# Weight preparation beside the matmuls: stores issued later, one shared ring of tiles, finer hand-out

## Chip, cores and metric

The kernel runs on one core of one Trainium2 chip. The metric is the device time of one execution in microseconds (us), lower is better. TensorE multiplies matrices, VectorE and ScalarE do element-wise work, GpSimd a few additions, and SyncE issues nearly all DMAs. In profiles they are PE (PEld its weight loads), DVE, ACT, POOL and SP (SPq its queue).

## The reference

Windowed attention, then a gated layer, then a second layer, all in float32 on 3072 tokens of width 512:

```python
# attention: 4 batches, 8 heads, 768 tokens, head dim 64, in chunks of 32 queries;
# keys: 8 memory keys, 16 to the left, the chunk, 8 to the right
a = np.exp(scores - max); a = a / (sum + 1e-9); out = a @ v_full
# gated layer, d_ff 1536
x = (sigmoid(x @ w_gate) * (x @ w_val)) @ w_out
# second layer, d_ff 2048
h = x @ w_in; out = (h * sigmoid(h)) @ w_out2
```

The weights arrive as 64-bit floats, and the kernel stages each weight as pairs of 32-bit words and makes its 32-bit value out of them.

## The kernel before

**Precision and products.** A float32 operand is split into an upper part (a cast on ScalarE) and a lower part (the difference, on VectorE); a product is three matmuls, upper x upper, upper x lower, lower x upper. Feature-major 128x512 tiles are multiplied by 128x128 weights.

**Gated layer** (the loop over `BLOCKS1`). Four blocks of 512 tokens, 12 rounds of 128 hidden features each. One round is 12 matmuls for the gate (`pg`), 12 for the value (`pv`), and 12 for the output of the round before (`emit_out1`). Three times a round, `steps(i)` runs attention's work that is due there (`run_events`) and lets the preparation go on. In the first block the gated layer's own weights are staged (`Feed`); from the second block on, output weights are reloaded from DRAM (`load_wo`), and `Pace` prepares operands. Attention has 24 tiles of 128 tokens. From tile 8 on, each takes two rounds: "meet" (context of the tile before, line 309, scores, line 221, maximum, subtraction and exponent, lines 258 to 270), two steps later "norm" (sum and reciprocal, lines 277 to 279, and eight ScalarE multiplications, line 286), four steps after the meet "turn" (four TensorE transposes, line 293, and a copy, line 294).

**Two more strips.** The last 1024 of the 3072 tokens pass the gated layer as the strip with index -1; then the second layer takes the 3072 tokens in three strips of 1024 (0, 1, 2). Both use a seven-product scheme on halves of each matrix, so their weights are needed as seven combined blocks. First products (`pair2`): each pair of hidden tiles takes seven products (A11, S1, S2, A12, S3, S4, A22, six matmuls each), summed into banks `c1`, `c2`, `c3`, which copies and additions (lines 980, 984, 922, 985) read between products: `c1` after product 1 by ScalarE, `c3` after product 2 by ScalarE, `c2` after products 3 and 5 by VectorE. Strip -1 has six pairs, each with a gate half and a value half (the value half multiplies on VectorE, line 974); strips 0 to 2 have eight pairs. After an odd pair a closing subtraction and split is done in the next one (`tail`, `form`). Then come second products (`out2`). The loads of combined weights (`next_granule`, five buffers) are issued as each buffer is used up.

**Preparation.** The combined weights are made on the chip and stored to DRAM. `PairC` makes those of the gated layer (gate, value, and output weights "o"), `Pair2` those of the second layer: of the input weights in the gated layer's blocks 1 to 3, of the output weights in the first products of strips -1 and 0. A `Pair2` loads two tiles (`stg`), changes the exponent range of their upper words on ScalarE ("rebias", line 125), joins words on VectorE (lines 135 and 138), makes four sums (line 627), and then for four operand tiles an upper part (ScalarE, line 97), a lower part (VectorE, line 100) and a store (lines 728 and 734). `prepare` is a generator over these pieces, each with an assumed cost; `Pace.go(us)` adds to a budget and takes pieces until it is spent. In the gated layer it gets 1.8 us per step, less attention's share; in the strips 3.0 after each half pair (`PREPC`) or pair (`PREPL`). Staged tiles have a ring of four; operand tiles have three buffers in the gated layer and two in the strips. A store is issued right behind its lower part. For an output weight of the gated layer, `reach` starts the pair when its even member is about to be multiplied, and line 668 adds the upper and lower parts of both members.

All engines run their queues in order, and the order is the one in which the program issues (`manual_schedule`).

Of the kernel before, what the change touches and what calls it, by code (L numbers as in the profile page):

```python
# [51 lines left out]
DVE_US = {"meet": 2.1, "norm": 1.0}  # L52
PREP1 = 1.8
PREPC = 3.0
PREPL = 3.0
# [3 lines left out]
def moe_kernel(ctx: ExitStack, tc: tile.TileContext, qh, kh, vh, wg, wv, wo, w2i, w2o, out):  # L59
# [52 lines left out]
    class Unit:  # L112
        def __init__(self, src, name, slot=None, keep=None):
            self.src, self.name, self.slot, self.keep = src, name, slot, keep
            self.pool = None

        def load(self):
            pool = self.pool or p1
            self.stg = pool.tile([P, 512, 2], I32, tag="stg", name=f"stg_{self.name}", bufs=4)
            return nc.sync.dma_start(out=self.stg.rearrange("p a b -> p (a b)"), in_=self.src)  # L120
# [267 lines left out]
    with tc.manual_schedule():  # L388
# [197 lines left out]
        events = {}  # L586
        for t in range(n0, NTILE + 1):
# [30 lines left out]
        def sums_of(f32s, order):  # L618
            at = {o: n for n, o in enumerate(order)}
            for o, a, b, op in (  # L620
# [5 lines left out]
                o, a, b = at[o], at[a], at[b]  # L626
                nc.vector.tensor_tensor(out=f32s[:, o], in0=f32s[:, a], in1=f32s[:, b], op=op)

        def co_tile(pool, name, bufs):
            co = pool.tile([P, 2, 512], F32R, tag="co", name=name, bufs=bufs)  # L630
            return co.rearrange("p a (m k) -> p a m k", m=2)

        class PairC:
# [3 lines left out]

            def load(self):
                if self.k != "o":
                    self.src = [w_t[2 * self.p + j][:, "gv".index(self.k)] for j in range(2)]  # L640
                    return
                self.src = None

            def early(self):
                return (1 + self.p % 2, 2 * self.p + 1) not in wo_u
# [13 lines left out]
            def steps(self):  # L659
                if self.k == "o":  # L660
                    bi = 1 + self.p % 2
                    even, odd = (wo_u[bi, 2 * self.p + j] for j in range(2))
                else:
                    even, odd = self.src
                f32s = p1.tile([P, 8, 256], F32, tag="f", name=f"fc{self.k}{self.p}")
                v = f32s.rearrange("p m c -> p (m c)")
                for o, w in ((v[:, :512], even), (v[:, 1536:], odd)):
                    nc.vector.tensor_tensor(
                        out=o, in0=w[:, 0].bitcast(F32), in1=w[:, 1].bitcast(F32), op=ALU.add
                    )  # L670
                if self.k == "o":
                    order = (A11, A21, S1, S2, S3, S4, A12, A22)
                else:
                    self.store(A11, even)
                    order = (A11, A12, S1, S2, S3, S4, A21, A22)
                    self.store(A22, odd[:, :, 256:])
                yield 1.4
                sums_of(f32s, order)
                yield 1.45
                for c, ids in enumerate(((S1, S2), (S3, S4))):  # L680
                    co = co_tile(p1, f"cc{self.k}{self.p}_{c}", 3)
                    split(co[:, 0], co[:, 1], f32s[:, 2 + 2 * c : 4 + 2 * c], nc.vector)
                    yield 0.7
                    if self.k == "o":
                        for n, i in enumerate(ids):
                            self.store(i, co[:, :, n])
                    else:
                        self.store(ids[0], co)

        class Pair2:  # L690

            def __init__(self, k, p, pool, bufs):
                self.k, self.p, self.pool, self.bufs = k, p, pool, bufs
                w = w2i if k == "i" else w2o
                self.units = [Unit(w[f], f"w2{k}{f}") for f in (2 * p, 2 * p + 1)]
                for u in self.units:
                    u.pool = pool

            def early(self):
                return False  # L700

            def load(self):
                for u in self.units:
                    u.load()

            def steps(self):
                k, p = self.k, self.p
# [12 lines left out]
                sums_of(f32s, range(8))  # L720
                yield 1.45
                for c in range(4):
                    m = min(2, 7 - 2 * c)
                    co = co_tile(self.pool, f"co{k}{p}_{c}", self.bufs)[:, :, :m]
                    split(co[:, 0], co[:, 1], f32s[:, 2 * c : 2 * c + m], nc.vector)
                    yield 0.7 if m == 2 else 0.4
                    if k == "i":
                        nc.sync.dma_start(
                            out=w2i_d[p, :, c // 2, :, 2 * (c % 2) : 2 * (c % 2) + m],
                            in_=co.bitcast(F32),  # L730
                        )
                    else:
                        for j in range(m):
                            nc.sync.dma_start(
# [562 lines left out]
```

## Time and profile before

| | us |
|---|---|
| median of 3 runs | 1213.25 (1208.88 to 1215.08) |
| the profiled execution | 1213.65, span 1211.9 |
| TensorE busy | 1125.5 |
| VectorE / ScalarE / GpSimd busy | 764.0 / 563.1 / 70.0 |

The profile is of one execution. "Busy" is the time in which an engine executes; in a line of waits, the engine before the arrow stood idle until the one behind it released it. In rows of the timeline the bracket at the end gives the idle time just before and what ended it. The granted clock (PEclk) is TensorE's, 1.00 for the higher of two levels.

### The profile page before, as it was taken

What the parts mean: (1) busy time and instruction counts of PE and PEld (TensorE: products, weight loads), DVE (VectorE), ACT (ScalarE), POOL (GpSimd) and SP (SyncE); (2) the same over time, 40 slices, a digit from 0 to 9 for tenths busy, and PEclk for the clock granted to TensorE, in tenths of its full rate; (3) what the DMA queues carried; (4) which work ended last, traced back from release to release, by engine and by line L of the source; (5) the groups of instructions that cost most, each with busy time, mean ns of one, the idle gap of its engine ahead of it and who ended that gap; (6) DMA issues with size and microseconds to landing.
All of it is one profiled execution on the core that took longest, in us unless ns stands there. A gap on an engine that the chain in (4) does not pass through costs nothing. (4 is left out here: it accounts for less than half of the span.)

```text
span 1211.9 us, 19021 instructions
## 1 busy us (share of the span) xinstructions
PE 1125.5 (93%) x7580; PEld 904.8 (75%) x7580; DVE 764.0 (63%) x1140; ACT 563.1 (46%) x919; POOL 70.0 (6%) x50
## 2 busy tenths in 40 slices
PE   7999999998899999877888996789999999999998
PEld 4888877776787777765666785668888888888887
DVE  7888756675566666455465974436873468734565
ACT  6766655554546553322223553335534445444442
POOL 0000000000000000011010101110001100011000
PEclk9999999998999999988888998889999999999999
DMA  8887777786676977656678767567575575755552
GB/s 300 286 296 271 242 274 251 261 274 235 241 260 236 342 270 269 211 196 212 234 261 272 263 220 240 165 203 292 187 247 183 191 302 178 246 194 186 224 198 95
DMA packets 106248, 288.03 MB, mean 238 GB/s; under 512 B 8624, under 2 KB 39344, under 8 KB 95408
## 3 DMA queue, kind: packets, MB, share of 16 engines
q1 hardware_dynamic: 105872, 286.43, 68.0%
q8 instruction: 60, 0.98, 0.3%
q10 hardware_dynamic: 288, 0.39, 0.1%
q14 instruction: 28, 0.23, 0.1%
HBM read 210.24 MB, written 76.55 MB: 237 GB/s over the span
## 5 line engine op out<-in xcount | busy, mean ns | idle before, releaser
L957 PE MATMUL c<-xp,wr 128*128 128x512 f32 x1008 | 237.6, 398 | 22.1 <-ACT s L980 20.2
L957 PEld LDWEIGHTS c<-xp,wr 128*128 128x128 f32 x1008 | 193.6, 193 | 65.5 <-ACT s L980 21.4
L1089 PE MATMUL o<-gf,wr 128*128 128x512 f32 x1008 | 229.0, 389 | 0.0
L1089 PEld LDWEIGHTS o<-gf,wr 128*128 128x128 f32 x1008 | 189.2, 188 | 39.3
L360 PE MATMUL pv<-x,w 128*128 128x512 f32 x564 | 143.8, 405 | 5.3 <-DVE sg L375 5.3
L360 PE MATMUL pg<-x,w 128*128 128x512 f32 x564 | 136.7, 391 | 1.3 <-ACT x L97 1.3
L100 DVE TENSOR_TENSOR gf<-g,gf 128x1024 fp32r<-128x1024 f32 x84 | 103.8, 1239 | 47.5 <-ACT gf L97 47.0
L360 PEld LDWEIGHTS pv<-x,w 128*128 128x128 f32 x564 | 107.1, 194 | 31.7 <-DVE sg L375 8.5
L97 ACT CAST gf<-g 128x1024 fp32r<-128x1024 f32 x84 | 88.1, 1052 | 86.8 <-PE o L1089 71.5
L360 PEld LDWEIGHTS pg<-x,w 128*128 128x128 f32 x564 | 104.9, 188 | 24.9 <-ACT x L97 3.5
L922 DVE TENSOR_TENSOR s<-c,s 128x512 f32<-128x512 f32 x48 | 33.2, 691 | 71.3 <-PE c L957 71.3
L377 ACT CAST g<-sg 128x512 fp32r<-128x512 f32 x48 | 29.8, 620 | 96.4 <-DVE sg L375 96.4
L97 ACT CAST coo<-fo 128x512 fp32r<-128x512 f32 (+1 forms) x32 | 17.5, 562 | 101.5 <-DMA w2o_d<-coo 67.8
L928 ACT ACTIVATE g<-s 128x512 f32<-128x512 f32 x48 | 30.3, 632 | 60.8 <-DVE s L922 60.8
L925 DVE TENSOR_TENSOR g<-g,g 128x1024 f32<-128x1024 f32 x48 | 58.4, 1216 | 0.0
L985 POOL TENSOR_TENSOR s<-s,s 128x512 f32<-128x512 f32 x24 | 37.4, 1559 | 348.2 <-ACT s L984 297.3
L100 DVE TENSOR_TENSOR coo<-fo,coo 128x512 fp32r<-128x512 f32 (+1 forms) x32 | 19.4, 623 | 53.6 <-ACT coo L97 53.6
L380 DVE TENSOR_TENSOR g<-sg,g 128x512 fp32r<-128x512 f32 x48 | 33.1, 689 | 24.8 <-ACT g L377 24.8
L286 ACT ACTIVATE e<-e,r 128x64 f32<-128x64 f32 x136 | 34.4, 335 | 28.4 <-DVE r L279 28.3
L922 DVE TENSOR_TENSOR u<-c,s 128x512 f32<-128x512 f32 x24 | 16.5, 688 | 39.9 <-PE c L957 38.0
L105 PE MATMUL y<-g,wor 128*128 128x512 f32 x144 | 40.1, 400 | 0.0
L270 ACT ACT_TABLE_LOAD x21 | 26.9, 1283 | 25.8 <-DVE e L262 23.9
(593 smaller groups left out, 1647.7 us busy)
## 6 DMA issues: line engine op xcount, KB each, us to landing
wr<-w2o_d SPq DMA_DIRECT2D x42, 1024.0 KB, 4.8
wr<-w2i_d SPq DMA_DIRECT2D x24, 1024.0 KB, 5.5
wor<-wo_d SPq DMA_DIRECT2D x36, 512.0 KB, 6.0
wr<-w2i_d SPq DMA_DIRECT2D x24, 768.0 KB, 4.5
w2o_d<-coo SPq DMA_DIRECT2D x56, 256.0 KB, 4.5
w2i_d<-coi SPq DMA_DIRECT2D x24, 512.0 KB, 3.8
wr<-wc_d SPq DMA_DIRECT2D x12, 1024.0 KB, 6.0
v<-in_vh_dram SPq DMA_DIRECT2D x21, 512.0 KB, 6.3
```

The source lines that it names most:

```text
L97: nc.scalar.copy(hi, src)
L100: lo_eng.tensor_tensor(out=lo, in0=src, in1=hi.bitcast(F32), op=ALU.subtract)
L105: nc.tensor.matmul(o, w_hi, x_hi, start=first, stop=False)
L286: nc.scalar.activation(out=e[:, g], in_=e[:, g], func=AF.Copy, scale=r[:, g])
L360: nc.tensor.matmul(o[:, :n], w[:, pw, kt * P : (kt + 1) * P], x[kt][:, px, :n], start=i == 0, stop=i == len(steps) - 1,)
L380: nc.vector.tensor_tensor(out=g[:, 1, :n], in0=sg[:, :n], in1=g[:, 0, :n].bitcast(F32), op=ALU.subtract)
L922: nc.vector.tensor_tensor(out=o, in0=a, in1=b_, op=ALU.add)
L925: nc.vector.tensor_tensor(out=o, in0=a, in1=b_, op=ALU.subtract)
L928: nc.scalar.activation(out=o, in_=i, func=AF.Silu)
L957: nc.tensor.matmul(o, w[:, pw, m, kt * P : (kt + 1) * P], X[i][:, px, kt], start=first and j == 0, stop=j == 5, skip_group_check=not first,)
L985: nc.gpsimd.tensor_tensor(out=s5, in0=s5, in1=s1, op=ALU.add)
L1089: nc.tensor.matmul(c[at[i], dp], w[:, pw, pl, dp * P : (dp + 1) * P], f[:, px, pl], start=i in (A11, S1, S2) and pp == 0 and j == 0, stop= ...
```

## The change

- **One ring.** Staged tiles and operand tiles share one tag: seven tiles in the gated layer, six in the strips (before, 4 + 3 and 4 + 2).
- **Late stores.** A store is put in a list behind its lower part and issued four calls of `go` later, or earlier if a new operand tile is asked for while four (in the strips three) stores are in the list.
- **Pieces apart.** After the rebias, and after the first upper parts, the call of `go` ends, so that joins and lower parts come at least one call later; upper parts are made two operand tiles ahead. The budget is held to 2.5 us. A pair's staged tiles are loaded behind the sums of the pair before.
- **Fine hand-out.** In the strips, `go(0.9)` is called inside `pair2` after every second product, in place of 3.0 after each pair.
- **Output weights of the gated layer.** `begin` adds both members when the odd one is about to be multiplied; the rest follows as the next item.
- **Attention.** From tile 8 on the exponent is issued one step after the subtraction, and the normalisation is one VectorE multiplication (line 288) instead of eight ScalarE ones. Assumed costs and budgets are set anew.

```diff
-DVE_US = {"meet": 2.1, "norm": 1.0}
-PREP1 = 1.8
-PREPC = 3.0
-PREPL = 3.0
+DVE_US = {"meet": 2.1, "norm": 1.75}
+PREP1 = 1.95
+PREP2 = 0.9
...
+                if fast:
+                    events.setdefault(at + 1, []).append(("exp", t))
...
-                        steps += list(att_scores(t, sx, e_tile(t)))
+                        more = list(att_scores(t, sx, e_tile(t)))
+                        if t >= 2 * n0:
+                            exps[t] = more.pop()
+                        steps += more
...
+                elif what == "exp":
+                    exps.pop(t)()
...
-                    att_norm(t, nc.scalar if t >= 2 * n0 else nc.vector)
+                    att_norm(t)
...
         def co_tile(pool, name, bufs):
-            co = pool.tile([P, 2, 512], F32R, tag="co", name=name, bufs=bufs)
-            return co.rearrange("p a (m k) -> p a m k", m=2)
+            co = pool.tile([P, 512, 2], I32, tag="stg", name=name, bufs=bufs)
+            co = co.rearrange("p a b -> p (a b)").rearrange("p (h m k) -> p h m k", h=2, m=2)
+            return co.bitcast(F32R)
...
+            def begin(self, even, odd):
+                self.t = [t_slot(f"tc{self.p}_{j}") for j in range(2)]
+                self.whole(self.t[0], even)
+                self.whole(self.t[1], odd)
...
         class Pair2:
...
-                for j, u in enumerate(self.units):
-                    u.rebias()
+                for u in self.units:
+                    u.rebias()
+                yield None
...
-                sums_of(f32s, range(8))
-                yield 1.45
+                sums_of({i: f32s[:, i] for i in range(8)})
+                if self.after is not None:
+                    self.after.load(pace)
+                yield 1.5
+                cos = []
+
+                def high(c):
+                    m = min(2, 7 - 2 * c)
+                    co = pace.co(self.pool, f"co{k}{p}_{c}")[:, :, :m]
+                    nc.scalar.copy(co[:, 0], f32s[:, 2 * c : 2 * c + m])
+                    cos.append(co)
+
+                high(0)
+                high(1)
+                yield None
                 for c in range(4):
-                    m = min(2, 7 - 2 * c)
-                    co = co_tile(self.pool, f"co{k}{p}_{c}", self.bufs)[:, :, :m]
-                    split(co[:, 0], co[:, 1], f32s[:, 2 * c : 2 * c + m], nc.vector)
-                    yield 0.7 if m == 2 else 0.4
...
+                    lo_of(cos[c], f32s[:, 2 * c : 2 * c + cos[c].shape[2]])
+                    pace.later(lambda c=c, co=cos[c]: self.store(c, co))
+                    if c + 2 < 4:
+                        high(c + 2)
+                    yield 0.7 if c < 3 else 0.4
...
         class Pace:
+            LAG = 4
...
+            def co(self, pool, name):
+                while len(self.fifo) >= self.cap:
+                    self.fifo.pop(0)[1]()
+                return co_tile(pool, name, self.bufs)
+
+            def later(self, store):
+                self.fifo.append((self.step, store))
...
             def go(self, us):
-                self.due += us
...
+                self.step += 1
+                while self.fifo and self.fifo[0][0] <= self.step - self.LAG:
+                    self.fifo.pop(0)[1]()
+                self.due = min(self.due + us, 2.5)
+                while self.due > 0:
+                    cost = self.advance()
+                    if cost is None or cost is False:
                         break
+                    self.due -= cost
+
+            def begin(self, item, *args):
+                item.begin(*args)
+                self.due -= 1.4
+                self.urgent.append(item)
...
                 if i in final:
                     next_granule()
+                if b < 0 or b == 0 and p < NPAIR - 2:
+                    beats[0] += 1
+                    if beats[0] % 2 == 0:
+                        prep.go(PREP2)
...
-                    if pending[0] in (1, 2) and pending[1] % 4 == 2 * pending[0] - 2:
-                        prep.reach(("o", pending[1] // 2))
+                    if pending[0] in (1, 2):
+                        seen[pending[1]] = wo_u[pending]
+                        if pending[1] % 4 == 2 * pending[0] - 1:
+                            q = pending[1] // 2
+                            prep.begin(PairC("o", q), seen[2 * q], seen[2 * q + 1])
...
-        prep = Pace([Pair2("o", p, pool, 2) for p in range(NPAIR)])
+        prep = Pace([Pair2("o", p, pool) for p in range(NPAIR)], 6, 3)
```

## Rows read from the trace of the kernel before

**Rows 1.** Page, first part: an engine's busy time, share of the span, instructions.
```profile
PE 1125.5 (93%) x7580; PEld 904.8 (75%) x7580; DVE 764.0 (63%) x1140; ACT 563.1 (46%) x919; POOL 70.0 (6%) x50
```
**Rows 2.** Table by stage: from:to and length, busy us, then granted clock, DMA share, GB/s.
```profile
149.76:486.29 336.53, 318.03 (x3106) 250.17 (x3105) 213.11 (x403) 173.73 (x341) 0.00 (x0) 0.98 0.75 265
494.44:661.67 167.23, 133.98 (x517) 105.20 (x516) 89.69 (x143) 49.01 (x87) 18.94 (x12) 0.90 0.69 238
661.67:720.43 58.76, 57.62 (x254) 47.38 (x253) 54.05 (x55) 31.31 (x35) 4.28 (x2) 1.00 0.69 232
720.43:827.13 106.70, 84.64 (x338) 67.60 (x337) 43.21 (x66) 39.02 (x65) 13.46 (x8) 0.87 0.64 209
827.13:1208.06 380.93, 380.92 (x1681) 314.89 (x1679) 232.93 (x236) 167.59 (x213) 32.64 (x22) 1.00 0.60 211
```
**Rows 3.** Chain that ended last, in order of time: start us, us, what.
```profile
730.83 9.50 DMA w2o_d<-coo
...
740.66 1.23 ACT stg_w2o L125 x2
...
903.29 76.16 PE c L957 x336
```
**Rows 4.** TensorE's waits: us in total, times, longest us.
```profile
PE c L957 <- ACT s L980: 20.2, 3, 8.4
PE sx L309 <- ACT at L294: 5.9, 2, 3.6
...
PE c_-1_5v L957 <- ACT s_-1_5v L980: 5.2, 1, 5.2
```
**Rows 5.** All engines' waits: us in total, times, longest us.
```profile
ACT coo L97 <- DMA w2o_d<-coo: 67.8, 10, 11.2
```
**Rows 6.** Timeline of TensorE in the gated layer: start us, us, instructions merged.
```profile
149.76 2.88 PE L360 MATMUL pg<-x,w 128*128 128x512 f32 x12
158.42 2.88 PE L360 MATMUL pg<-x,w 128*128 128x512 f32 x12
168.55 2.88 PE L360 MATMUL pg<-x,w 128*128 128x512 f32 x12
...
486.29 2.88 PE L360 MATMUL pg<-x,w 128*128 128x512 f32 x12
```
**Rows 7.** Waits of the stretch 140 to 494 us.
```profile
PEld pt L293 <- ACT e L286: 14.8, 43, 0.5
```
**Rows 8.** Timeline of the gated layer.
```profile
152.07 2.02 ACT L286 ACTIVATE e<-e,r 128x64 f32<-128x64 f32 x8 [1.86 <-DVE r L279]
...
282.57 0.69 DVE L668 TENSOR_TENSOR fco<-wor 128x512 f32<-128x512 f32 x1 [7.97 <-DMA wor<-wo_d]
...
288.56 5.38 PE L360 MATMUL pv<-x,w 128*128 128x512 f32 x12 [1.30 <-DVE sg L375]
```
**Rows 9.** Page, DMA issues: KB each, median us from issue to landing.
```profile
w2o_d<-coo SPq DMA_DIRECT2D x56, 256.0 KB, 4.5
```
**Rows 10.** Groups by line and shape, 494.2 to 827.1: busy us, mean ns; idle before.
```profile
L100 DVE TENSOR_TENSOR coo<-fo,coo 128x512 fp32r<-128x512 f32 x24 | 15.9, 688 | 30.8 <-ACT coo L97 30.8
...
L135 DVE TENSOR_SCALAR stg_w2o<-stg_w2o 128x512 int32<-128x512 int32 x16 | 6.8, 422 | 5.5 <-DMA stg_w2o<-in_w2o_dram 5.5
...
L925 DVE TENSOR_TENSOR g<-g,g 128x1024 f32<-128x1024 f32 x3 | 3.7, 1217 | 0.0
```
**Rows 11.** Timeline of strip -1's first products.
```profile
513.07 0.69 ACT L125 ACTIVATE stg_w2o<-stg_w2o 128x512 f32<-128x512 f32 x1 [4.83 <-DMA stg_w2o<-in_w2o_dram]
...
572.74 1.71 POOL L985 TENSOR_TENSOR s_-1_2v<-s_-1_2v 128x512 f32<-128x512 f32 x1 [9.75 <-ACT s_-1_2v L984]
...
573.34 2.52 DVE L627 TENSOR_TENSOR fo<-fo 128x256 f32<-128x256 f32 x4
...
608.80 1.54 DVE L627 TENSOR_TENSOR fo<-fo 128x256 f32<-128x256 f32 x4
```
**Rows 12.** Table by stretch, columns as in rows 2: the densest five us.
```profile
410.00:415.00 5.00, 4.07 (x139) 3.18 (x138) 4.15 (x9) 1.40 (x4) 0.00 (x0) 1.00 1.04 404
```

More of the change, by code (lines that the diff above doesn't have):

```diff
@@ L636, in __init__ @@
                 self.k, self.p = k, p
[L638 to L645, printed above, removed]
             def store(self, idx, part):
@@ L657, in store, with whole @@
                     nc.sync.dma_start(out=out, in_=part)
[L659 to L664, printed above, removed]
+            def whole(self, o, w):
+                nc.vector.tensor_tensor(
+                    out=o, in0=w[:, 0].bitcast(F32), in1=w[:, 1].bitcast(F32), op=ALU.add
+                )
+            def begin(self, even, odd):
+                self.t = [t_slot(f"tc{self.p}_{j}") for j in range(2)]
+                self.whole(self.t[0], even)
+                self.whole(self.t[1], odd)
@@ L665, in steps @@
+            def steps(self, pace):
                 f32s = p1.tile([P, 8, 256], F32, tag="f", name=f"fc{self.k}{self.p}")
                 v = f32s.rearrange("p m c -> p (m c)")
[L667 to L670, printed above, removed]
+                at = {i: f32s[:, 2 + n] for n, i in enumerate((S1, S2, S3, S4))}
                 if self.k == "o":
-                    order = (A11, A21, S1, S2, S3, S4, A12, A22)
-                else:
+                    t = [x.rearrange("p (m c) -> p m c", m=2) for x in self.t]
+                    at.update({A11: t[0][:, 0], A21: t[0][:, 1], A12: t[1][:, 0], A22: t[1][:, 1]})
+                else:
+                    even, odd = (w_t[2 * self.p + j][:, "gv".index(self.k)] for j in range(2))
+                    at.update({A11: f32s[:, 0], A12: f32s[:, 1], A21: f32s[:, 6], A22: f32s[:, 7]})
+                    self.whole(v[:, :512], even)
+                    self.whole(v[:, 1536:], odd)
@@ L696, in __init__, with load, store @@
+            def load(self, pace):
                 for u in self.units:
[L697 to L702, printed above, removed]
+                    u.pool, u.bufs = self.pool, pace.bufs
+                    u.load()
+            def store(self, c, co):
+                k, p, m = self.k, self.p, co.shape[2]
+                if k == "i":
+                    nc.sync.dma_start(
+                        out=w2i_d[p, :, c // 2, :, 2 * (c % 2) : 2 * (c % 2) + m],
+                        in_=co.bitcast(F32),
+                    )
+                else:
+                    for j in range(m):
+                        nc.sync.dma_start(
+                            out=w2o_d[ORDER2.index(2 * c + j), p // 4, :, p // 2 % 2, :, p % 2],
+                            in_=co[:, :, j].bitcast(F32),
+                        )
@@ L719, in steps @@
                     yield 1.15
-                sums_of(f32s, range(8))
-                yield 1.45
-                for c in range(4):
-                    m = min(2, 7 - 2 * c)
-                    co = co_tile(self.pool, f"co{k}{p}_{c}", self.bufs)[:, :, :m]
-                    split(co[:, 0], co[:, 1], f32s[:, 2 * c : 2 * c + m], nc.vector)
-                    yield 0.7 if m == 2 else 0.4
[L727 to L734, printed above, removed]
-                                out=w2o_d[ORDER2.index(2 * c + j), p // 4, :, p // 2 % 2, :, p % 2],
-                                in_=co[:, :, j].bitcast(F32),
-                            )
@@ L770, in finish @@
             def finish(self):
[L771 removed]
+                while self.advance() is not False:
+                    pass
+                while self.fifo:
+                    self.fifo.pop(0)[1]()
         g_t, wo_u, yacc = {}, {}, {}
```

103 lines of the change are left out of this document (51 added, 52 removed).

## Prediction

> **What bounds the kernel now.** I read the share of busy time first: TensorE is busy 93% of the span [rows 1], so only TensorE's lost time can be won, and the question is where it lies. The table by stage answers that [rows 2]. Its lines are: the gated layer with attention beside it (most of three of its four blocks), the first products of the strip at index -1, the second products of that strip, the first products of strip 0, and all the rest. In the rest TensorE is busy 380.92 of 380.93 us at a granted clock of 1.00, and 336 matmuls take 76.16 us there [rows 3], so 0.2267 us each. That is the yardstick for full speed.
>
> By it, strip -1's first products (12 half pairs of 42 matmuls, and 12 of the gated layer's last output) need 516 x 0.2267 = 117.0 us and took 167.23: 50.3 lost. Its second products need 252 x 0.2267 = 57.1 and took 58.76: 1.6 lost. Strip 0's first products need 76.16 and took 106.70: 30.5 lost. In these two first-product stages the second layer's output weights are prepared; their later twins, with the same products and no preparation, lose nothing.
>
> The list of TensorE's waits says who ended them: ScalarE's copy at line 980, three times for 20.2 us in strip 0 and six times in strip -1, for up to 5.2 us [rows 4]. That copy stands in ScalarE's queue behind the upper-part cast of a prepared weight, and the list of all waits has that cast waiting 67.8 us for stores of earlier operands to land [rows 5]. The chain of waits shows one case whole: a store under way for 9.50 us, behind it (past the cast) the rebias of the next pair, 1.23 us [rows 3], and only then the copy that TensorE waits for. The operand tiles have two buffers there, so a third operand waits for the first one's store; and the preparation comes in blocks of 3 us between half pairs, so nothing else on ScalarE gets past. The granted clock of the two stages is 0.90 and 0.87 [rows 2], which lies in the losses above.
>
> In the gated layer, 33 rounds, counted between two first matmuls of a round [rows 6], took 336.53 us [rows 2]; at full speed a round of 36 matmuls is 8.16 us, so 67.2 us are over. Part of this is attention's own work on TensorE. A round with an unhindered transpose took 158.42 - 149.76 = 8.66 (0.50 over), the next, with scores and context, 10.13 (1.97 over) [rows 6]; 15 tiles x 2.47 = 37. So 30 us are lost, in two main places. The transposes wait 43 times for ScalarE's eight per-head normalisations, 14.8 us on the weight loads [rows 7], where an unhindered tile waits for none: some 12 us on TensorE. And VectorE stands 7.97 us for a reload of an output weight [rows 8], twice, which holds up attention's copy (TensorE 5.9 us [rows 4]) and the gate; afterwards 12 matmuls take 5.38 us [rows 8], against 2.88 [rows 6], the lower of the two clock levels. That is some 13 us with the clock. About 5 are scattered.
>
> **The change, part by part.** *Ring and late stores, second layer.* Operand tiles share one ring of six with the staged weights, and a store is issued four hand-outs later. In the two first-product stages a hand-out comes after every second product (6 matmuls each, so every 2.72 us). I counted the budget through the code: 0.9 per hand-out, 63 hand-outs, against eight weight pairs of 6.3 each. One pair takes seven hand-outs, 14 products, and all are done at product 112 of 126. In steady state the 14 products, gate half then value half, carry: after gate product 2 one join, after 4 the other, after 6 the sums, three late stores and the next two loads, after value product 1 the fourth store, after 3 two casts, after 5 two casts and three low parts, after 7 the last low part and the next rebias. The first casts come four products (5.4 us) after the hand-out of the stores that they wait for, and SyncE gets to these up to two products sooner, as its last wait before them is for gate product 4: a lead of 5.4 to 8.1 us. The low parts follow two products later, 2.7 us more. A store's median landing is 4.5 us [rows 9]; the one of the chain took 9.50. So ScalarE's wait nearly ends, and what remains lies in the value half, where ScalarE has only two copies to make. On SyncE's queue stores pass behind operand loads that wait for TensorE, as now, but no store waits for VectorE any more, and the loads behind them go sooner.
>
> *Fine hand-out.* The pieces cost the same: a join 0.42 + 0.69 us, a low part 0.69 [rows 10], four sums 1.54 [rows 11]. VectorE is busy 89.69 of 167.23 us [rows 2]; at full speed the same work fills 77%. What counts is the two tight additions of each half pair: products 5 and 7 write to a bank that VectorE must have read within the product before, 1.36 us, of which the addition takes 0.69. In the value half, counted from product 4's end, VectorE multiplies (0.69), makes three low parts (2.06) and then adds (0.69): 3.44, against two products, 2.72. TensorE waits 0.72 us, six times: 4.3 us. After an odd value half, counted from product 7's end, come an addition, a multiplication, the last low part (under 0.69), the closing subtraction and split (2 x 1.22 [rows 10]), a join and the tight addition: 6.3 to 6.7 against four products, 5.44, about 1.2 late, twice: 2.4 us. At the start the rebias stands ahead of a copy and waits for the first staged weights; now that load landed at 513.07, with ScalarE idle for 4.83 us [rows 11]. The new one is issued earlier but needed earlier: I keep 4.5. With 1.5 for late landings the stage keeps 12.7, say 13, of 50.3: **37 won**. Its bounds are 5 kept (only the start) and 25 (each of the six low-part groups 2 us later, for a landing). Strip 0 has no multiplication on VectorE; two such groups and three closings at under 1 us each: it keeps 4 of 30.5 (1 to 10), **26 won**. Second products: 0.
>
> *Gated layer.* The normalisation goes to VectorE, whose 128x512 operations take 0.69 us [rows 10]: 15 tiles, 10.4 us more on an engine busy 213.11 of 336.53 (then 71% of 316), two hand-outs ahead of the transposes. ScalarE loses 15 x 2.02 = 30 us [rows 8]. With the exponent a step later ScalarE no longer stands before VectorE's subtraction. Those 12 us go. The whole output weights are added when the odd one is about to be multiplied, so both have landed, and the 13 us go. New are bursts on VectorE of up to 3.8 us (two joins and the sums in one hand-out), and some nine casts for which the cap of four forces a store early, so that they may wait for its landing, some 4 us; a gate or an output has two groups of twelve matmuls, 5.4 us, of slack. I let 5 us stay for these, and the 5 scattered: **20 won** of 30, bounds 10 and 27.
>
> **Sum.** 20 + 37 + 26 = 83 of the profiled 1213.65 us (the median of the runs is 1213.25, so nothing is shifted): 1130.65, **1131 us**. With all lower residues 27 + 45 + 29.5 = 101.5 and 1112; with all upper ones 10 + 25 + 20.5 = 55.5 and 1158.
>
> **A rule that speaks against it.** The four sums took 2.52 us where a GpSimd addition (572.74 to 574.45) ran beside them and 1.54 where none did [rows 11]: 1 us more. The Trainium skill, page SBUF — State Buffer, section "SBUF: two separate sides", gives the cause: a VectorE instruction with two inputs in SBUF and a GpSimd one take turns on a port pair, and whoever starts first keeps it for the whole instruction. By that rule the finer hand-out would make 1139 of the 1131; the trace agrees with it.
>
> **The rivals.** (1) *Landing still rules.* Less waiting makes the DMA queue denser: per 14 products 6400 KB move, in 19 us 344 GB/s, where the stage has 238 now [rows 2] and the densest five us 404 at a DMA share of 1.04 [rows 12]. For it: that is 85% of the peak. Against it: the four to six products of lead. If each of the eight weight pairs loses 2.75 us more, 22 us: 1153. (2) *The port.* A join after gate product 2 falls into the window of GpSimd's addition; if each of eight loses the 1 us of [rows 11] ahead of a tight addition, 8 us: 1139. (3) *VectorE becomes the gated layer's bound* and nothing is won there: 1151. (4) *Slower.* Preparation stands in front of the tight additions everywhere: 18 half pairs x 2 = 36 places. The 83 us are gone at 2.3 us a place, more than the largest burst (2.06), and then the low clock follows each. At 2.6 a place, 94 us: 1225. Against it: only one such burst in 14 products. (5) *It doesn't do what it says*: the casts wait for the ring's staged loads instead of the stores, and all stays: 1213.
>
> **Chances.** Forecast 0.62, (1) 0.15, (2) 0.09, (3) 0.09, (4) 0.03, (5) 0.02. A measurement can tell about 0.5% from no change. Faster 0.95, same 0.02, slower 0.03. The range 1110 to 1160 takes in the bounds of the sum and (1) to (3).
>
> **What would show it.** In the profile after: ScalarE's waits for the output weights' stores fall from 67.8 us to under 15; TensorE's waits for line 980 vanish but for the start, those for VectorE's additions rise to about 10 us, none over 2; the first-product stages take about 130 and 80 us at clocks over 0.95; the transposes wait for no normalisation, and VectorE for no output weight. It is wrong if casts still wait for landings, if VectorE's additions hold TensorE for over 20 us, or if the gated layer's 336 us stay.

## The result, and the profile after

The changed kernel takes 1138.37 us (median of 4 runs, 1136.6 to 1139.58), the kernel before, run beside it, 1214.16: a ratio of 0.9382, 95% interval 0.935 to 0.9414. The forecast was 1131 in a range of 1110 to 1160. The profiled execution spans 1137.8 us against 1211.9, so 74.1 us are to be explained.

The first view is the same as [rows 1], on the page after: each engine's busy time. TensorE's fell by 28 us for the same 7580 matmuls, most of what the lower clock had cost (a run below that never left the higher one needs 39 less than the kernel before); the other 46 us of the gain were idle time.

```profile
PE 1097.2 (96%) x7580; PEld 893.0 (78%) x7580; DVE 772.7 (68%) x1156; ACT 534.9 (47%) x791; POOL 66.7 (6%) x50
```

The table by stage, with the columns and the five stages of [rows 2]:

```profile
149.99:463.76 313.77, 304.88 (x3106) 247.97 (x3104) 224.55 (x422) 143.98 (x218) 0.00 (x0) 0.99 0.81 281
471.92:608.54 136.62, 124.64 (x518) 99.40 (x516) 90.41 (x150) 52.35 (x90) 17.09 (x12) 0.96 0.81 282
608.54:666.97 58.43, 57.45 (x253) 47.22 (x252) 51.77 (x49) 31.65 (x36) 4.28 (x2) 1.00 0.71 246
666.97:753.02 86.05, 78.92 (x338) 64.06 (x337) 42.95 (x65) 37.17 (x61) 11.96 (x8) 0.98 0.77 266
753.02:1133.95 380.93, 380.93 (x1681) 314.89 (x1679) 232.93 (x236) 167.67 (x213) 32.64 (x22) 1.00 0.60 211
```

Against [rows 2] the gated layer won 22.8 us, the first products of strip -1 won 30.6, those of strip 0 20.7; the second products (0.3) and the rest did not move. So all three stages that were forecast to win did, and two of the three won less than forecast (20, 37 and 26).

What still stands in the way is in the list of TensorE's waits after (us in total, times, longest):

```profile
PE pg L361 <- ACT x L96: 6.2, 1, 6.2
PE c_-1_2g L1005 <- DVE u_-1_2g L970: 3.4, 1, 3.4
PE c L1005 <- DVE u L970: 3.3, 1, 3.3
PE c_-1_4g L1005 <- DVE u_-1_4g L970: 3.1, 1, 3.1
PE c L1005 <- DVE s L970: 2.3, 1, 2.3
PE c_-1_0g L1005 <- ACT s_-1_0g L1036: 2.0, 1, 2.0
...
PE c L1005 <- ACT s L1032: 1.5, 1, 1.5
...
PE c_-1_5v L1005 <- DVE s_-1_5v L970: 1.2, 1, 1.2
```

ScalarE's copy (line 980 before, 1032 after) held TensorE in strip 0 for 20.2 us in [rows 4] and does so for 1.5 now. In its place stand a few single waits of 2 to 3 us, and one of 6.2 us in the gated layer. All but the one of 2.0 us, at the start of strip -1, shrink or go in the run below that issues its stores at once. In the list of all waits after, and among the page's landings:

```profile
ACT coo L754 <- DMA w2o_d<-coo: 34.7, 16, 5.4
...
ACT cco L691 <- DMA w2i_d<-coi: 5.2, 1, 5.2
ACT ccg L691 <- DMA w2i_d<-coi: 5.0, 2, 3.5
```

```profile
w2o_d<-coo SPq DMA_DIRECT2D x56, 256.0 KB, 6.3
```

The cast of the output weights' upper parts waits half of its 67.8 us [rows 5] still, and the median landing of their stores rose from 4.5 [rows 9] to 6.3 us. The timeline of strip -1's first products shows one such case from end to end (start us, us, engine, line, instruction; in brackets the idle time before and what ended it):

```profile
510.85 0.44 SPq L954 DMA_DIRECT2D wr<-wc_d  x1
...
511.35 0.50 SPq L724 DMA_DIRECT2D w2o_d<-coo  x1
...
511.56 1.29 POOL L1037 TENSOR_TENSOR s_-1_1v<-s_-1_1v 128x512 f32<-128x512 f32 x1 [8.18 <-ACT s_-1_1v L1036]
...
513.97 0.62 ACT L754 CAST coo<-fo 128x512 fp32r<-128x512 f32 x1 [0.77 <-DMA w2o_d<-coo]
...
519.97 0.41 ACT L754 CAST coo<-fo 128x256 fp32r<-128x256 f32 x1 [5.38 <-DMA w2o_d<-coo]
...
523.49 2.07 POOL L1037 TENSOR_TENSOR s_-1_2g<-s_-1_2g 128x512 f32<-128x512 f32 x1 [10.63 <-ACT s_-1_2g L1036]
...
524.35 1.49 DVE L136 TENSOR_SCALAR stg_w2o<-stg_w2o 128x512 int32<-128x512 int32 x1
...
526.48 0.68 DVE L970 TENSOR_TENSOR u_-1_2g<-c_-1_2g,s_-1_2g 128x512 f32<-128x512 f32 x1
...
527.22 1.66 PE L1005 MATMUL c_-1_2g<-xp-1_3_5371,wr 128*128 128x512 f32 x6 [3.36 <-DVE u_-1_2g L970]
...
528.72 2.70 PE L1005 MATMUL c_-1_2g<-xp-1_6_5433,wr 128*128 128x512 f32 x6
```

The chain of waits that ended last has the same store with its landing (start us, us, what):

```profile
511.35 8.55 DMA w2o_d<-coo
```

The last store of a weight pair is issued at 511.35 and its tile is wanted at 514.59, when the third cast of the next pair ends. The fourth cast starts at 519.97, after 5.38 us of idle ScalarE. Behind it the rebias, the copies and GpSimd's addition all come late, the addition runs beside a join whose first step takes 1.49 us instead of the 0.42 of [rows 10], and the tight addition at line 970 reaches TensorE 3.36 us too late. Six matmuls then take 2.70 us instead of 1.52. The granted clock of that stretch is 0.50, the lower of TensorE's two levels (columns as in the table by stage):

```profile
528.80:532.20 3.40, 3.40 (x10) 2.63 (x9) 2.81 (x6) 0.65 (x2) 0.00 (x0) 0.50 1.12 390
```

### The profile page after: what moved, and what is told of

The parts are those of the page before. It is cut to its first block, busy times and chain, and to the rows that moved or that the text cites. A ratio compares the mean times of both kernels' runs of the same rounds, so it can differ in the third digit from the quotient of the medians.

```text
span 1137.8 us, 18863 instructions
## 1 busy us (share of the span) xinstructions
PE 1097.2 (96%) x7580; PEld 893.0 (78%) x7580; DVE 772.7 (68%) x1156; ACT 534.9 (47%) x791; POOL 66.7 (6%) x50
## 4 chain that ended last, share of the span: by engine, by line
PE 84%; DMA 8%; DVE 5%; ACT 1%; SPq 1%; issue 0%; ACTq 0%; DVEq 0%
PE o L1141 20%; PE c L1005 19%; PE pg L361 11%; PE pv L361 10%; DMA w2o_d<-coo 5%; PE y L104 3%; PE y L106 3%; PE y L108 3%; PE sx L310 1%; PE sx L222 1%; PE o_-1_1_6471 L1141 1%; PE o_-1_0_6470 L1141 1%; PE pt L294 1%; PE c_-1_3g L1005 1%; PE c_-1_1g L1005 1%; PE c_-1_0v L1005 1%
## 5 line engine op out<-in xcount | busy, mean ns | idle before, releaser
L1005 PE MATMUL c<-xp,wr 128*128 128x512 f32 x1008 | 231.7, 391 | 7.1 <-DVE u L970 3.3
L1005 PEld LDWEIGHTS c<-xp,wr 128*128 128x128 f32 x1008 | 189.9, 189 | 48.4 <-DVE u L970 3.7
L361 PE MATMUL pv<-x,w 128*128 128x512 f32 x564 | 139.0, 395 | 2.1 <-DVE sg L376 2.0
L361 PEld LDWEIGHTS pv<-x,w 128*128 128x128 f32 x564 | 103.9, 188 | 26.3 <-DVE sg L376 3.0
L371 ACT ACTIVATE sg<-pg 128x512 f32<-128x512 f32 x48 | 28.6, 597 | 28.8 <-PE pg L361 28.6
L104 PE MATMUL y<-g,wor 128*128 128x512 f32 x144 | 40.0, 400 | 0.0
L106 PE MATMUL y<-g,wor 128*128 128x512 f32 x144 | 38.7, 390 | 0.0
L108 PE MATMUL y<-g,wor 128*128 128x512 f32 x144 | 38.6, 390 | 0.0
```

The source lines that it names most:

```text
L104: nc.tensor.matmul(o, w_hi, x_hi, start=first, stop=False)
L106: nc.tensor.matmul(o, w_hi, x_lo, start=False, stop=False)
L108: nc.tensor.matmul(o, w_lo, x_hi, start=False, stop=last)
L361: nc.tensor.matmul(o[:, :n], w[:, pw, kt * P : (kt + 1) * P], x[kt][:, px, :n], start=i == 0, stop=i == len(steps) - 1,)
L1005: nc.tensor.matmul(o, w[:, pw, m, kt * P : (kt + 1) * P], X[i][:, px, kt], start=first and j == 0, stop=j == 5, skip_group_check=not first,)
```

## The experiments

Three parts of the change could be held against each other: the **late issue** of the stores, the **ring**, and the **order of the work** (steps apart, fine hand-out, normalisation on VectorE, addition at the odd weight). My theory after the result was that what is still lost hangs on the late issue of a pair's last store.

All runs in one table. "Start" is the first matmul of strip -1's first products, so it measures the gated layer; the three lengths run from there to the first matmul of the next stage. All are read from TensorE's timeline. The kernel before stood between 1210 and 1215 us beside them, so 2 to 3 us between runs of different rows tell nothing by themselves.

| kernel | median us | ratio, 95% | start | first, -1 | second, -1 | first, 0 |
|---|---|---|---|---|---|---|
| before | 1214.16 | 1 | 494.44 | 167.23 | 58.60 | 106.70 |
| after | 1138.37 | 0.935 to 0.9414 | 471.92 | 136.62 | 58.43 | 85.89 |
| stores at once (e1_now) | 1110.87 | 0.9138 to 0.9194 | 460.43 | 128.45 | 57.12 | 78.28 |
| stores two later (e2_lag2) | 1120.84 | 0.9216 to 0.9275 | 467.39 | 128.45 | 57.12 | 79.52 |
| ring alone (e9_ring) | 1164.09 | 0.9575 to 0.9627 | 497.24 | 142.24 | 58.58 | 82.17 |
| hand-out in blocks (e3_block) | 1143.31 | 0.9402 to 0.9464 | 471.55 | 138.03 | 61.24 | 87.45 |
| normalisation back (e4_actnorm) | 1143.16 | 0.9396 to 0.9455 | 475.20 | 135.42 | 59.26 | 86.51 |
| early addition (e5_early) | 1136.82 | 0.9348 to 0.9397 | 467.94 | 137.08 | 58.35 | 87.04 |
| no GpSimd addition (e7_nopool) | 1131.15 | 0.9299 to 0.9378 | 471.24 | 129.93 | 58.31 | 83.79 |
| at once, one addition (e10_now_dve) | 1109.95 | 0.913 to 0.9173 | 461.44 | 126.27 | 57.14 | 78.50 |
| at once, steps joined (e11_now_fused) | 1123.54 | 0.9233 to 0.9264 | 463.28 | 136.16 | 57.12 | 80.62 |
| at once, three parts undone (e12_now_rest) | 1132.56 | 0.931 to 0.9338 | 473.44 | 132.70 | 57.67 | 82.94 |
| at once, all of these and the exponent (e13_now_both) | 1159.84 | 0.9537 to 0.9565 | 498.33 | 134.69 | 58.82 | 83.65 |
| as that, exponent apart (e14_now_exp) | 1155.75 | 0.9518 to 0.9589 | 493.76 | 132.12 | 58.85 | 83.67 |

**The late issue.** Stores at once:

```
     def later(self, store):
-        self.fifo.append((self.step, store))
+        store()
```

> The changed kernel, but each store is issued right behind its lower part, as before the change; ring, order of pieces, hand-out and attention stay as changed. If the late issue is what wins (SyncE then waits for VectorE at each store and holds back the loads behind it, and the ring's stores land too late), much of the 76 us comes back: 1160 or more, with SyncE's waits for VectorE at the stores back at over 60 us. If the larger ring and the order of the pieces win by themselves, the time stays within 5 us of the changed kernel's 1138, or falls, as stores land sooner.

1110.87 us: the late issue costs 27.5 us (26 by the two ratios). The ring and the order together win 100 to 103, by the kernel before that ran beside the one or the other. The second run issues them two hand-outs later instead of four (`LAG = 2`):

> The changed kernel with stores issued two hand-outs later instead of four, and nothing else. Theory: what the first-product stages still lose (19.6 and 9.9 us against full speed) hangs on the fourth store of each weight pair, which is issued 6 to 8 us before its buffer is wanted and lands 8.5 us after: the last cast waits 5.4 us, VectorE behind it, and TensorE 3.1 to 3.4 us at the additions of halves 2g and 4g. Two hand-outs sooner those waits fall under 1.5 us, strip -1's first products take 127 to 130 us instead of 136.6 and strip 0's 79 to 82 instead of 86.1; the 6.2 us wait at a block boundary of the gated layer (a cast behind a store that the cap forced out) should go too: 1118 to 1126 in all. Rival: the closing work and the join fill VectorE, with GpSimd on the shared port; then the stages keep their times within 2 us and the total is 1130 to 1139.

1120.84, between the two, as expected, and so are the two first-product stages. Two points of the expectation failed: the tight waits stayed at 1.7 us in strip -1 and 2.7 in strip 0, and TensorE's wait of 6.2 us in the gated layer fell to 4.2 but did not go. With stores at once none of ScalarE's waits for a prepared weight's store is left in the list; two later, 1.9 us are left for the output weights. The median landing is not shorter for that: 5.7 us at once, 7.0 at two, 6.3 at four. So it is the lead that decides, not the landing. The line of the run with two:

```profile
ACT coo L754 <- DMA w2o_d<-coo: 1.9, 2, 1.2
```

What the early stores were thought to hurt shows in the waits of SyncE's DMA queue at once:

```profile
SPq L718 <- DVE coi L641: 48.7, 17, 9.9
SPq L654 <- DVE cco L641: 32.0, 6, 10.7
...
SPq L828 <- DVE tc L663: 19.5, 6, 6.0
```

SyncE stands 80.7 us for VectorE's low parts in these two lines alone, and TensorE does not pay for it: its list of waits between 150 and 460 us has 0.5 us in all. SyncE's wait for the reload's tile (line 828) is 19.5 us, and was 57.0 with the late stores. The table by stage of the same run, for the gated layer and strip -1's first products, has the clock at 1.00 throughout:

```profile
149.99:452.27 302.28, 301.61 (x3101) 246.23 (x3100) 223.87 (x421) 143.02 (x218) 0.00 (x0) 1.00 0.83 292
460.43:588.88 128.45, 119.94 (x518) 96.07 (x517) 89.68 (x150) 54.70 (x95) 16.85 (x12) 1.00 0.89 310
```

**The ring.** The kernel before with nothing but one ring for staged weights and operands (seven tiles, then six; shortened):

```
-            co = pool.tile([P, 2, 512], F32R, tag="co", name=name, bufs=bufs)
+            co = pool.tile([P, 512, 2], I32, tag="stg", name=name, bufs=bufs)
```

> The kernel before with one part of the change alone: staged tiles and operand tiles in one ring of seven (strips: six); stores at once, order of pieces, blocks of 3 us and attention as before. If the two operand buffers of the strips were the bound, the first-product stages (167.2 and 106.7 us) lose at least half of their 80 us over full speed, 1165 to 1180 in all, and ScalarE's waits for the output weights' stores fall from 67.8 to under 20 us. If the order of the pieces is what counts, casts still stand in front of the copies and the gain stays under 20 us: 1192 or more.

1164.09: the ring alone wins about 49 us, nearly all in the two first-product stages (25.0 and 24.5), and nothing in the gated layer. No wait of a cast for an output weight's store is left in its list; the casts wait for VectorE's sums instead:

```profile
ACT coo L97 <- DVE fo L627: 31.8, 7, 9.5
```

So the ring does in strip 0 (82.17) what the whole changed kernel does not reach (85.89).

**The fine hand-out.** A half pair's hand-outs are given in one block after its last product:

```
-                    if beats[0] % 2 == 0:
-                        prep.go(PREP2)
+                    if beats[0] % 7 == 0:
+                        for _ in range(3 + beats[0] // 7 % 2):
+                            prep.go(PREP2)
```

> The changed kernel, but the three or four hand-outs of a half pair are made in one block behind its last product, in place of one behind every second product; ring, late stores and all else stay. If the fine hand-out is needed, blocks of VectorE work stand ahead of the closing and of the tight additions again: the two first-product stages lose 10 to 20 us more than the changed kernel's 29.5, 1148 to 1158 in all. If the ring and the late stores do the work, the stages keep their times within 4 us: 1134 to 1142.

1143.31, some 5 us more than 1138.37: between what the two theories expected, and little for the part that the name of the change ends with. ScalarE's waits for stores stay, 38.5 us.

**Normalisation and early addition**, each undone by itself (the second shortened):

```
-                    att_norm(t)
+                    att_norm(t, nc.scalar if t >= 2 * n0 else nc.vector)
```

> The changed kernel with the normalisation from tile 8 on back on ScalarE, eight operations a tile; the budgets and the exponent's later step stay as changed. If the transposes' waits for it were on TensorE's path, some 10 to 13 us come back in the gated layer (313.8 us there), 1148 to 1152 in all. If they were hidden behind another wait, under 4 us: 1137 to 1142.

```
-                        if pending[1] % 4 == 2 * pending[0] - 1:
+                        if pending[1] % 4 == 2 * pending[0] - 2:
+                            seen[2 * q + 1] = wo_u[pending[0], 2 * q + 1]
```

> The changed kernel, but the two members of an output weight of the gated layer are added when the even one is about to be multiplied, as before the change, the odd one perhaps still under way. If VectorE then stands for the reload again, twice some 8 us, 10 to 14 us come back: 1148 to 1153. If the reload was late only because SyncE stood at stores, which the late issue mends, it has landed by then: 1136 to 1141.

1143.16 and 1136.82: 4.8 us and nothing, where the prediction had 12 and 13. VectorE did not wait for a reload with the early addition either. But both ran under late stores, which hold the gated layer at other places, so they were tried again below.

**The port.** GpSimd's addition left out of the first products:

```
-            nc.gpsimd.tensor_tensor(out=s5, in0=s5, in1=s1, op=ALU.add)
```

> The changed kernel without GpSimd's addition of the first product's sum in the first products (24 additions of 128x512): that part of the computation is left out, its copies and VectorE's additions stay. If GpSimd's turn on a shared port is what delays VectorE's join in halves 2g and 4g (1.49 us instead of 0.42 for its first step), the waits of 3.4 and 3.1 us there shrink by at least 1 us each and the stages by 4 to 8 us: 1130 to 1134. If the late landing of the fourth store is behind them, they shrink by under 1 us each, as VectorE was late already: 1135 to 1138.

1131.15, 7.2 us less (5 by the ratios), as expected of the port; the two first-product stages are 6.7 and 2.1 us shorter. The timeline has the same join's first step at 0.42 us again:

```profile
521.78 0.42 DVE L136 TENSOR_SCALAR stg_w2o<-stg_w2o 128x512 int32<-128x512 int32 x1
```

TensorE's waits before the tight additions of strip -1 fell from 3.4 and 3.1 to 2.1 and 2.0 us, and the one for `u` in strip 0 from 3.3 to 2.2, not to nothing. The first two are 2.3 of the 6.7 us of strip -1; most of the rest is the clock, which was granted at 1.00 throughout that stage. On top of the stores at once, the copy and the addition were then made one VectorE addition in the gate halves of strip -1 and in strip 0 (the added lines):

```
+            if b <= 0 and kind != "v":
+                add(s5, c3, s1)
+            else:
+                nc.scalar.copy(s5, c3)
+                nc.gpsimd.tensor_tensor(out=s5, in0=s5, in1=s1, op=ALU.add)
```

> Stores at once, as in e1_now (1110.9), and in the gate halves of strip -1 and in strip 0 the first product's sum is added by one VectorE operation that reads the bank, in place of ScalarE's copy and GpSimd's addition. If GpSimd's turn on a shared port is the rest of the waits in halves 2g and 4g (1.6 and 1.7 us), strip -1's first products go from 128.5 to 124 to 126 us and strip 0's from 78.3 to 77: 1105 to 1109. If VectorE's own backlog is, 0.7 us more on it each half makes no gain: 1110 to 1114.

1109.95 us, 0.9 below 1110.87, which a measurement can't tell from nothing. Strip -1 is 2.2 us shorter, the gated layer 1.0 longer. So with the stores at once this exchange gains nothing. What the port alone still costs there was not separated, as the run also gives VectorE an operation of some 0.7 us in each of these halves.

**The order of the work, without the late stores.** Rebias and join, cast and low part put into one hand-out again (shortened):

```
-                high(0)
-                high(1)
-                yield None
                 for c in range(4):
+                    high(c)
                     lo_of(cos[c], f32s[:, 2 * c : 2 * c + cos[c].shape[2]])
```

> The kernel with stores issued at once (1110.87 us), and the steps of a preparation put together again: rebias with its join, each upper-part cast with its low part, in one hand-out, instead of a hand-out apart. Theory: with the landing out of the way, the spreading of the steps is what carries most of the gated layer's gain, since ScalarE and VectorE no longer wait for each other within one hand-out: 10 to 25 us come back, 1121 to 1136, most of it in the gated layer (302 us there now). Rival, as the prediction has it: the normalisation and the early addition carry it; then under 5 us come back, 1109 to 1116.

1123.54: 12.7 us come back, in the expected range, but not where it was expected: 2.9 in the gated layer, 7.7 in strip -1. Then the other three parts undone (the edits of the three runs above):

> Stores issued at once (1110.87 us), and three other parts undone together: the normalisation of the fast tiles back on ScalarE, the output weights added when the even one is due, and the strips' preparation in one block per half pair. Separately, with late stores, they gave back 4.8, 0 and 4.9 us. Theory (they are small and add up): 1116 to 1124, with the gated layer under 310 us. Rival, as the prediction sized them: 12 + 13 us of the gated layer come back, so that it takes over 322 us, and the time is 1136 or more.

1132.56: 21.7 us, 13.0 of them in the gated layer, 4.3 and 4.7 in the first products. Neither theory: twice the sum of the separate runs, and in the gated layer half of what the prediction had. Both together, with the exponent in the scores' step:

> Stores issued at once, the steps put together again, the three other parts undone, and the exponent back in the step of the scores: what is left of the change is the ring, the loads' place and the budget of a hand-out. The kernel before with the ring alone took 1164. Theory (all parts are found): 1145 to 1170, and the sum of what the two runs beside it gave back lies within 15 us of it. Rival: under 1135, then something not yet named (the loads' place or the budgets) carries the rest.

1159.84: 49.0 us come back, 14.6 more than 12.7 + 21.7, just inside the 15 expected. All parts are found to within some 4 us, as the ring alone stands at 1164.09. The gated layer holds the surplus: 37.9 us against 2.9 + 13.0. A last run put the exponent a step later again:

> As the run with the steps put together and the three other parts undone (1159.84), but with the exponent a step after the scores, as in the changed kernel. In the gated layer the joint steps alone gave back 2.9 us, the three other parts 13.0, all with the exponent 37.9: 22 are not accounted for. If the exponent's step carries them: strip -1 begins at 475 to 482 us and the time is 1136 to 1145. If the parts need each other (ScalarE is late only when normalisation and joint steps meet): strip -1 begins at 492 to 499 and the time is 1153 to 1162.

1155.75, strip -1 from 493.76, as expected of parts that need each other: most of the surplus stays without the exponent (33.3 us in the gated layer). Whether the exponent itself is worth the 4 us between the two medians can't be told, as the ratios are 0.9551 and 0.9554. So the parts need each other, and the waits of VectorE in the gated layer (150 to 452 us) show where. First with the three parts undone, steps apart:

```profile
DVE ccg L641 <- ACT ccg L691: 11.8, 3, 4.6
...
DVE ccv L641 <- ACT ccv L691: 9.1, 2, 4.6
DVE coi L641 <- ACT coi L754: 6.8, 2, 3.4
```

and with the steps joined as well:

```profile
DVE coi L641 <- ACT coi L750: 26.5, 10, 4.6
DVE ccv L641 <- ACT ccv L691: 22.9, 8, 4.6
...
DVE ccg L641 <- ACT ccg L691: 16.0, 6, 3.6
...
DVE cco L641 <- ACT cco L691: 7.6, 4, 3.6
```

The low parts wait 73.0 us for their own upper parts instead of 32.3 (with cco's 4.6). A joined step asks VectorE for the low part at once, while the cast stands behind 2 us of normalisation on ScalarE [rows 8]; what VectorE does for attention and the gate comes late with it. These waits are not the price by themselves: with the steps joined and nothing else undone they are 31.7 us, as many as with the three parts undone, and the one cost 2.9 us and the other 13.0. By which path they reach TensorE was not followed to the end. The transposes show the other end, first steps apart, then joined (weight loads, whole trace):

```profile
PEld pt L294 <- ACT e L287: 9.2, 22, 1.7
```

```profile
PEld pt L294 <- ACT e L287: 22.3, 48, 1.7
```

In the profile after, with the normalisation on VectorE and the steps apart, the weight loads of the transposes have no such wait in their list, and the matmuls wait 0.7 us for it in all.

## Why the prediction was right, and where it was off

The time came out 7 us above the forecast and inside the range. But the mechanism was only half right, and that two errors partly cancel is luck. By its own signs the prediction fails in two places: casts still wait for landings, and four of TensorE's waits for VectorE's additions are over 2 us, where none was to be. The transposes and the reload came out as it said.

**The late issue, wrong in sign.** The prediction took ring and late stores as one thing and put the whole 37 + 26 us to it and the fine hand-out. The ring wins; the late issue costs 27.5 us of that and of the gated layer. The step that failed is the lead: "a lead of 5.4 to 8.1 us", with "A store's median landing is 4.5 us [rows 9]" against it. The count of hand-outs was right, the two durations were not. The store was issued at 511.35 and wanted at 514.59, a lead of 3.2 us. It was late because SyncE's own issuing, which the prediction put at nothing, takes time: from 504.55 on SyncE issues without a break, first the six stores before it (4.64 us), then two staged loads and an operand load.

```profile
504.55 4.64 SPq L724 DMA_DIRECT2D w2o_d<-coo  x6
509.29 1.47 SPq L121 DMA_DIRECT2D stg_w2o<-in_w2o_dram  x2
```

And it landed 8.55 us after its issue, near the 9.50 of [rows 3], not near the median. An estimate from the counts shows that the median of after does no better: a pair takes 14 products of 1.36 us, 19.0 us, and its six tiles are the whole ring, so a tile comes up again after 19.0 us. It is held for one hand-out from cast to low part and four until the store, 5 x 2.72 = 13.6 us, and then for the landing: 19.9 at 6.3 us, 22.2 at 8.55. With two hand-outs it is 8.2 + 7.0 = 15.2, and with stores at once 2.7 + 5.7 = 8.4 and whatever VectorE is late. The first doesn't fit into 19.0, the other two do, and ScalarE's waits for the output weights' stores say the same (34.7, 1.9 and none). A larger ring with the late stores, which would test the estimate from the other side, was not run. The prediction's bound for ScalarE's store waits, 15 us, was thus missed.

**Strip -1's first products: 19.6 us kept, not 13.** Of the 13, the start was to keep 4.5 (TensorE waits 2.0), the value halves 4.3 (five waits of 0.5 and one of 1.2, 3.6 before rounding) and the two closings 2.4 (3.4 and 3.1, 6.5). TensorE's idle time, 136.62 - 124.64 = 12.0 us, is thus near the 12.7 of the sum, but by luck: closings with landings came out high and the start low. What was left out is the clock. Busy are 124.64 us, against 119.94 for the same products with stores at once at a clock of 1.00, so 4.7 us lie in it: the granted clock fell to 0.50 three times, just behind the waits of 2.0, 3.4 and 3.1 us. Strip 0 kept 9.7 instead of 4, with waits of 3.3, 2.3 and 1.5 us; with stores at once one of 1.6 is left of them.

**The gated layer: 22.8 won, forecast 20, for other reasons.** The forecast let 5 us stay for forced stores and bursts. The trace has one such place at 6.2 us of TensorE's wait. By the code the cap of four forces a store out at the boundary of two blocks, ScalarE's cast waits 5.21 us for the landing, and the split of the next block's x stands behind it. The timeline after:

```profile
239.96 0.38 SPq L718 DMA_DIRECT2D w2i_d<-coi  x1
...
247.53 0.62 ACT L691 CAST cco<-fco 128x512 fp32r<-128x512 f32 x1 [5.21 <-DMA w2i_d<-coi]
248.05 2.17 ACT L96 CAST x<-x 128x512 fp32r<-128x512 f32 x4
...
248.72 4.67 PE L361 MATMUL pg<-x,w 128*128 128x512 f32 x12 [6.23 <-ACT x L96]
```

Issuing two hand-outs later instead of four does not remove it: the same cast still waits 4.5 us for such a store and TensorE 4.2. The late stores cost 11.5 us in this layer (471.92 against 460.43), and without them it wins 34, which is above the prediction's upper bound of 27. So the forecast hit because the gain was sized too low and the late stores took a third of it. The normalisation's 12 us were a real mechanism: the transposes stopped waiting, and [rows 7] has its twin in the joined run (22.3 us, 48 times). But what it is worth hangs on the steps: undone by itself it cost 4.8 us, and the three parts undone together cost the gated layer 13.0 us with steps apart and 30.5 with steps joined; its own share of these was not measured. The 13 us for the reload were put to the wrong part: the wait of 7.97 us [rows 8] went away, and stayed away with the early addition in all four runs that had it, while the ring alone keeps it (14.9 us in three waits). What sends the reload sooner (the place of the pair's loads, the end of the waiting for a due pair) was not separated.

**The rivals.** The landing (rival 1, 0.15) was the one that came true in part: its cause was put to a denser queue and should have been put to the lead. With stores at once strip -1 moves 310 GB/s, more than the 282 after, and no cast waits for a store. The port (rival 2) came true at about its price, 5 to 7 us against 8, as long as late stores made the steps collide, though the 1 us a place that it was made of gives some 3 us at three places; most of the rest is clock. The Trainium skill, page SBUF — State Buffer, section "SBUF: two separate sides", also counts VectorE operations in a two-port mode among those that take turns with GpSimd. The trace agrees: a one-input operation took 1.49 us beside the addition and 0.42 without it. VectorE as the gated layer's bound (rival 3) did not come: it was busy 224.55 of 313.77 us. Nothing of rivals 4 and 5 was seen.

**What moved where, in sum.** From 1214: the ring to 1164; loads' place, budgets and the exponent together to 1156, about; steps apart, normalisation, addition and fine hand-out together to 1111 (12.7 and 21.7 when undone singly, the rest only jointly); the late issue back up to 1138. Of the three in the 21.7 us the shares were not separated. The best kernel here is the changed one with stores at once, 1110.87 us, or 1109.95 with the single addition.

## What to carry to other kernels

For a store from a ring, add up how long a tile is held, from its first write to the landing, and hold that against the time in which the ring comes round; delay the issue only by what is left over, and count with the landings of the busy stage rather than the median of the whole kernel. Count the issuing queue's own time too: here six stores took 4.64 us to go out. A queue that stands waiting need not cost anything: look at who waits for what is behind it before moving anything out of its way. And undo parts together as well as singly, as here two groups of parts that were worth 16 us of the gated layer apart were worth 33 together.

## What the runs showed of the hardware

That a store of 256 KB landed 8.55 us after its issue in a stage moving 282 GB/s, where the median of the kernel before was 4.5 us. That an int32 VectorE operation with one input, 128x512, took 1.49 us beside a GpSimd addition, which itself took 2.07 us instead of 1.29, and 0.42 us when it had none beside it. That six stores of 256 KB took SyncE 4.64 us to issue. And that TensorE's granted clock fell to 0.50 just behind single waits of 1.98, 3.36 and 3.10 us in one run, while in others it stayed at 1.00 behind waits of 1.93 us (stores at once), 2.68 (two later) and 2.81 (exponent apart). The length of the one wait does not tell.
